# Query split, group norm and the filter's spectrum split on GpSimd instead of VectorE, with other filler pacing, in a kernel for attention and a spectral filter

## The chip, the cores and the metric

The kernel runs on one core of a Trainium2 chip. A core has five engines, each with an instruction stream of its own: TensorE (PE in the profile; its weight loads, PEld, overlap its matmuls), VectorE (DVE), ScalarE (ACT), GpSimd (POOL) and SyncE (SP, which here only issues DMAs). On-chip data lies in SBUF; TensorE writes to PSUM, eight banks of 128 x 512 f32 here. The engines meet through semaphores only, and DMAs move data beside them.

The metric is the device time of one execution in microseconds, the median of several runs. Lower is better.

## What is computed

Two results stand side by side in the output of 2048 rows. On the left is attention with 16 query heads of 28 columns over one shared head of keys and values, then the output projection; on the right a filter in the frequency domain (a two-dimensional real FFT, a product with learned weights, the inverse).

```python
q = (x @ wq).reshape(B, S, H, Dh).transpose(0, 2, 1, 3)    # S 2048, H 16, Dh 28
k = x @ wk
v = x @ wv
scores = jnp.einsum("bhqd,bkd->bhqk", q, k) * (Dh ** -0.5)
p = softmax(scores, axis=-1)
o = jnp.einsum("bhqk,bkd->bhqd", p, v)
a = o.transpose(0, 2, 1, 3).reshape(B, S, H * Dh) @ wo
X = jnp.fft.rfft2(x2, axes=(-2, -1)) * (w_r + 1j * w_i)    # x2 is 2048 x 448
b = jnp.fft.irfft2(X, s=(S, D), axes=(-2, -1))
out = jnp.concatenate([a, b], axis=-1)
```

## The kernel before, in words

**Attention.** The 2048 queries are four chunks c of 512, the 16 heads four groups g of 4, the 2048 keys 16 blocks kc of 128. The main loop has 256 steps, one for each (c, g, kc), in that order. In a step TensorE makes the scores of four heads in two pairs (`scores`, L1257), ScalarE takes the exponential of each pair (L1260, 128 x 1024), and TensorE adds the product with the values into the group's bank (`values`, L1276). Two banks take the groups by turns: the values of a group can't start until VectorE has emptied the bank of the group two before.

**What follows a group.** `group_out` (L1151, VectorE) takes the finished bank out into `qraw`, in the place of the queries that it came from, and GpSimd issues two DMAs that bring the rows of softmax sums through DRAM into `rs` (L1156, L1157). `group_sums` takes the reciprocal (L1161, VectorE) and has GpSimd spread it over `R` (L1162, four L1164). `group_norm` (from L1172) multiplies by `R` and splits the result into a high and a low f16 half, `oh` and `ol`: three VectorE operations of 512 columns. After a chunk's fourth group, SP's DMAs L1184 and L1185 place rows of low parts into spare rows of `oh` and `ol`, and the chunk's output projection (`w_unit`, matmuls L1195, taken out by L1200) may be issued.

**What precedes a group.** `build_q` makes the next group's queries: `split_q` (L207 to L209, three operations of 512 columns) masks them and splits them into f16 halves `qh` and `ql`, then SP writes both to DRAM (L215) and reads them back four times, stacked as the score matmuls want them (L218, `qa`). `split_q` also stands in a branch that these inputs do not take.

**The filter.** Its parts are filler between the attention's steps. On TensorE: the late features and late points of the forward transform (`late_features` out by L1013, `late_points` matmul L1026, out by L1035), then, in the last third, eight spectral products (`z_unit`, L1094), each followed by the last transform (`y_unit`, L1120, out from L1127). Between the two stands VectorE's work on the whole spectrum `X`: a transform over 32 points (`forward`, `inverse`), whose butterflies are pairs of 904 columns (`plain`, L817 and L818), quarter turns (L835 and the four operations behind it, the first of them L837) and general ones (L852, L859), with the product with the filter (L933) in the middle. `X` comes through DRAM: each late point ends in SP's stores t<-bs (`fft1_store`, L196), and after the last one `spectrum` queues the four last loads of `X` (`spread`, L802) on GpSimd, the peak's round trip on SP (`bounce`, L911 and L913, back in L916) and all butterflies as background work of VectorE. After the inverse, `store` (L973) writes `X`, `fft3_load` (L1066) and `fft3_ready` (L1075) bring a product's spectrum and factors in on GpSimd's queue, and `fft3_split` (L1080, L1081) scales and splits the spectrum into f16 halves `c2`, two VectorE operations of 904 columns.

**What sets the order.** Each engine runs its instructions in the order in which they were written, and the kernel writes them by a small model of three clocks (`clk` of TensorE, VectorE, ScalarE). `after(when, dur, f)` books a piece of work: when VectorE's modelled clock has passed `when`, `vector` writes it and moves that clock on by `dur`. Background work is taken where nothing is booked. GpSimd and SP have no clock of their own; what `f` writes on their queues falls in wherever `f` is called. Filler on TensorE is rationed: each step adds to `owed`, and `fill` writes a unit where `owed` is positive. In the early part a step adds the first number of `EARLY`, from the last late point to the opening of the last stage the second, and then what is left spread over the remaining steps. All filler of the early part together, or of the late part, is the same whatever the numbers; they move where it stands.

The prologue (matmul L339, splits such as L533, copies L595, maxima L616) lies ahead of the loop; L1362 and L1365 normalise and split the last group behind it.

## Time and profile before

| | |
|---|---|
| median of 3 runs | 580.23 us (580.09 to 580.28) |
| the profiled execution | 580.55 us, its span 578.8 |
| granted TensorE clock | 0.999 |
| score matmuls L1257 | 4096, 275.5 us |
| value matmuls L1276 | 2048, 268.0 us |
| takings-out of a group, L1151 | 15, 11.3 us, 750 ns each |
| DMA to or from HBM | 44.22 MB read, 19.97 MB written, 111 GB/s |

The profile is of one execution. Busy times of an engine are shares of its span of 578.8 us; the execution's own time is 1.75 us longer than the span. An engine's row gives busy us, share and count of instructions, a group's row count, then busy us and mean ns of one, and behind the bar the idle time ahead of its instructions with what ended it. A timeline row is start, duration, engine, line and operation, with count and idle time ahead; SPq and POOLq are the DMA issues. A window row is the window, its length, then for PE, PEld, DVE, ACT and POOL the busy time (with the number of instructions), then the granted clock, the share of DMA time and its rate in GB/s. A row of the chain is start, duration, engine, tile, line and count.

### The profile page before, as it was taken

What the parts mean: (1) busy time and instruction counts of PE and PEld (TensorE: products, weight loads), DVE (VectorE), ACT (ScalarE), POOL (GpSimd) and SP (SyncE); (2) the same over time, 40 slices, a digit from 0 to 9 for tenths busy, and PEclk for the clock granted to TensorE, in tenths of its full rate; (3) what the DMA queues carried; (4) which work ended last, traced back from release to release, by engine and by line L of the source; (5) the groups of instructions that cost most, each with busy time, mean ns of one, the idle gap of its engine ahead of it and who ended that gap; (6) DMA issues with size and microseconds to landing.
All of it is one profiled execution on the core that took longest, in us unless ns stands there. A gap on an engine that the chain in (4) does not pass through costs nothing.

```text
span 578.8 us, 20617 instructions
## 1 busy us (share of the span) xinstructions
PE 570.6 (99%) x8941; PEld 295.8 (51%) x8941; DVE 390.5 (67%) x747; ACT 513.3 (89%) x580; POOL 102.6 (18%) x187
## 2 busy tenths in 40 slices
PE   9999899999999999999999999999999999999997
PEld 7877454545554444444444444445455555555544
DVE  5996717955421999999898887854366743366544
ACT  3743899999999999999999999998999887898982
POOL 1023311312103011122111111133201221011110
PEclk9999999999999999999999999999999999999999
DMA  8864681625516102242211020467224341212111
GB/s 296 291 212 126 178 267 49 189 84 139 168 35 219 57 19 66 74 123 97 91 34 57 22 79 26 147 220 211 97 89 127 107 131 70 89 58 74 41 56 65
DMA packets 38333, 66.27 MB, mean 115 GB/s; under 512 B 6724, under 2 KB 28532, under 8 KB 38232
## 3 DMA queue, kind: packets, MB, share of 16 engines
q1 hardware_dynamic: 29792, 39.13, 20.9%
q0 software_dynamic: 8304, 25.58, 13.9%
q8 instruction: 70, 1.15, 0.8%
q10 hardware_dynamic: 144, 0.23, 0.1%
q14 instruction: 23, 0.19, 0.1%
HBM read 44.22 MB, written 19.97 MB: 111 GB/s over the span
## 4 chain that ended last, share of the span: by engine, by line
PE 72%; issue 7%; DVE 6%; DMA 3%; POOL 1%; ACT 1%; POOLq 0%; DVEq 0%; ACTq 0%
PE banks L1257 31%; PE banks L1276 30%; PE banks L1195 6%; PE banks L1094 2%; PE banks L1120 2%; DMA rd<-rs 1%; DMA wf<-w 1%; DVE X L817 1%; DVE X L818 1%; DMA R<-rd 1%; PE banks L1026 1%; DVE X L859 1%; PE banks L173 0%; ACT yb L1207 0%; DVE w L852 0%
## 5 line engine op out<-in xcount | busy, mean ns | idle before, releaser
L1260 ACT ACTIVATE p<-banks 128x1024 f32<-128x1024 f32 x512 | 477.4, 1095 | 24.7 <-PE banks L1257 23.4
L1257 PE MATMUL banks<-qa,ka 128*32 128x512 f16 x4096 | 275.5, 379 | 1.6 <-ACT p L1260 1.1
L1276 PE MATMUL banks<-p,vs 128*32 128x512 f32 x2048 | 268.0, 592 | 0.0
L1257 PEld LDWEIGHTS <-ka 128*32 128x32 f16 x4096 | 127.4, 96 | 169.9 <-issue 121.0
L1276 PEld LDWEIGHTS banks<-p,vs 128*32 128x32 f32 x2048 | 68.7, 110 | 44.6 <-issue 1.8
L1156 POOL DMA_DIRECT2D sd<-qraw x15 | 10.1, 676 | 204.5 <-DVE qraw L1151 204.5
L1195 PE MATMUL banks<-woh,o 128*32 128x448 f16 x464 | 39.5, 353 | 0.7 <-DVE X L837 0.7
L1164 POOL DMA_DIRECT2D R<-rd x60 | 30.6, 518 | 42.3 <-DMA rd<-rs 37.0
L1195 PEld LDWEIGHTS <-o 128*32 128x32 f16 x720 | 21.5, 97 | 29.0 <-issue 20.9
L859 DVE SCALAR_TENSOR_TENSOR X<-w,X 128x226 f32<-128x226 f32 (+2 forms) x72 | 34.1, 474 | 2.4
L1151 DVE TENSOR_SCALAR qraw<-banks,scales 128x512 f32<-128x512 f32 x15 | 11.3, 750 | 33.8 <-PE banks L1276 33.8
L1200 DVE TENSOR_SCALAR ya<-banks,scales 128x448 f32<-128x448 f32 x12 | 8.2, 684 | 27.8 <-PE banks L1195 27.8
L1127 DVE TENSOR_SCALAR w<-banks,scales 128x256 f32<-128x256 f32 x16 | 7.8, 484 | 27.3 <-PE banks L1120 27.3
L1162 POOL DMA_DIRECT2D rd<-rs x15 | 8.2, 550 | 92.4 <-DVE rs L1161 83.7
L1195 PE MATMUL banks<-wol,o 128*32 128x448 f16 x256 | 24.0, 352 | 0.0
L339 PE MATMUL banks<-xh,wqh 128*128 128x512 f32 x64 | 23.6, 399 | 0.0
L339 PE MATMUL banks<-xh,wql 128*128 128x512 f32 x64 | 23.0, 389 | 0.0
L343 ACT ACTIVATE qraw<-banks 128x512 f32<-128x512 f32 x16 | 9.3, 594 | 14.8 <-PE banks L339 14.8
L817 DVE TENSOR_TENSOR X<-X 128x904 f32<-128x904 f32 (+2 forms) x10 | 9.1, 906 | 15.6 <-DMA X<-t 15.6
L852 DVE SCALAR_TENSOR_TENSOR w<-X 128x113 f32<-128x113 f32 (+2 forms) x56 | 17.8, 356 | 0.1
L339 PE MATMUL banks<-xl,wqh 128*128 128x512 f32 x48 | 17.2, 390 | 0.0
L933 DVE TENSOR_TENSOR w<-X,wf 128x904 f32<-128x904 f32 x16 | 17.0, 1096 | 0.2
(155 smaller groups left out, 531.5 us busy)
## 6 DMA issues: line engine op xcount, KB each, us to landing
qa<-qd SPq DMA_DIRECT2D x62, 128.0 KB
ob<-yo SPq DMA_DIRECT2D x16, 256.0 KB
t<-bs SPq DMA_DIRECT2D x16, 226.0 KB
w<-w POOLq DMA_DIRECT2D x8, 452.0 KB, 4.7
X<-t POOLq DMA_DIRECT2D x8, 452.0 KB, 7.0
wf<-w POOLq DMA_DIRECT2D x8, 452.0 KB, 5.0
x<-t POOLq DMA_DIRECT2D x8, 452.0 KB, 5.0
R<-rd POOLq DMA_DIRECT2D x60, 56.0 KB, 2.1
```

The lines of the kernel that those rows point to most:

```text
L339: mm(pq[c, g], w[:, j, gs], x[:, j], start=(j == 0 and n == 0), stop=(j == 3 and n == 1))
L817: todo(226 * n, lambda: TT(both(a), both(a), both(b), op=ALU.add), at)
L852: STT(out, y, sy, x, op0=ALU.mult, op1=ALU.add if c > 0 else ALU.subtract)
L859: todo(226 * n, lambda d=d, q=q: STT(both(d), t[0].rearrange("p r n f -> p r (n f)"), q, both(a), op0=ALU.mult, op1=ALU.add))
L933: TT(u[r], both(s), wt[k][:, r:r + 1].to_broadcast([128, 2, 452]), op=ALU.mult)
L1094: mm(pz[r, j], fb["c2", q % 2][:, x, e, j, r], fb["fi", q % 2][:, j, f], start=(n == 0), stop=(n == 2))
L1120: mm(py[m:m + 32, k].rearrange("p (j n) -> p j n", j=4), cs3[:w, kind, f, m:m + 32], fb["z", q % 2, e][:w, x, :, 64 * r:64 * r + 64], star ...
L1164: nc.gpsimd.dma_start(R[32 * i:32 * i + DH], rd[i:i + 1].to_broadcast([DH, CW]))
L1195: mm(p[r:r + 32], x[c][:, g, s][:, r:r + 32], w[:, m], start=(g == 0 and n == 0), stop=(g == NG - 1 and n == 2))
L1257: mm(bank[b + h][r], ka[:, k:k + 32], qa[c, g][:, 2 * p + h], start=True, stop=True)
L1260: nc.scalar.activation(pt[i], banks[:, b:b + 2], AF.Exp, scale=SCALE / UP / UP)
L1276: mm(bank[b][32 * i:32 * i + 32], vs[:, kc], pt[2 * st + i // 2][:, i % 2], start=(kc == 0), stop=(kc == 15))
```

## The change

Three pieces of work are written for GpSimd instead of VectorE. `build_q` hands `split_q` GpSimd as its engine (the branch that isn't taken keeps VectorE). `group_norm` issues its multiply, copy and subtract on GpSimd. `fft3_split` does so too, and in three operations where it had two: the spectrum is scaled in place, then copied to the high half, then subtracted for the low half. None of the three moves VectorE's modelled clock any more (their durations become 0.0), and two delays grow: output projections are released 10 modelled us after a chunk's last norm instead of 7, and a spectral product 6.0 after its split instead of 0.2. `EARLY` goes from 0.22 to 0.18 in its first number, so the early filler is spread over more steps. From `fft3_split` on, a line's number is one higher than before.

```diff
--- before.py
+++ after.py
@@ -33,7 +33,7 @@
 TOP = 61440.0
 ROW = 32768.0
 DUE = 50.0
-EARLY = 0.22, 0.13
+EARLY = 0.18, 0.13
 PEAK = 16384.0
 LAG = 0.45
 BOUND = float(np.float32(40.0 / SCALE * UP * UP / ROW / 4))
@@ -202,11 +202,11 @@
 
     qa, qd = {}, {}
 
-    def split_q(qt, qh, ql, c, g):
+    def split_q(qt, qh, ql, c, g, eng=nc.vector):
         cs = slice(c * CW, (c + 1) * CW)
-        nc.vector.tensor_scalar(qt, qraw[:, g, cs], mask, cvec[:, g, c:c + 1], op0=ALU.mult, op1=ALU.add)
-        nc.vector.tensor_copy(qh, qt)
-        nc.vector.tensor_tensor(ql, qt, qh, op=ALU.subtract)
+        eng.tensor_scalar(qt, qraw[:, g, cs], mask, cvec[:, g, c:c + 1], op0=ALU.mult, op1=ALU.add)
+        eng.tensor_copy(qh, qt)
+        eng.tensor_tensor(ql, qt, qh, op=ALU.subtract)
 
     def stack_out(n, p, src, eng):
         if p == 0:
@@ -220,7 +220,7 @@
     def build_q(c, g):
         qt = qp.tile([128, CW], F32, name="qt")
         qh, ql = (qp.tile([128, CW], F16, name=f"q{n}") for n in "hl")
-        split_q(qt, qh, ql, c, g)
+        split_q(qt, qh, ql, c, g, nc.gpsimd)
         for p, src in enumerate((qh, ql)):
             stack_out(4 * c + g, p, src, nc.sync)
         for p in range(4):
@@ -1073,13 +1073,14 @@
     def fft3_ready(q):
         if q < 8:
             nc.gpsimd.dma_start(fb["fi", q % 2], t["fi"][:, 4 * q:4 * q + 4])
-            after(max(clk["dve"], landed[q]), 2.3, fft3_split, q)
+            after(max(clk["dve"], landed[q]), 0.0, fft3_split, q)
 
     def fft3_split(q):
         x, c2 = fb["x", q % 2], fb["c2", q % 2]
-        V.tensor_scalar(c2[:, 0], x, scale_x, None, op0=ALU.mult)
-        STT(c2[:, 1], x, scale_x, c2[:, 0], op0=ALU.mult, op1=ALU.subtract)
-        after(clk["dve"] + 0.2, 0.0, work["z"].extend, [z_unit(q, 0), z_unit(q, 1)])
+        nc.gpsimd.tensor_scalar(x, x, scale_x, None, op0=ALU.mult)
+        nc.gpsimd.tensor_copy(c2[:, 0], x)
+        nc.gpsimd.tensor_tensor(c2[:, 1], x, c2[:, 0], op=ALU.subtract)
+        after(clk["dve"] + 6.0, 0.0, work["z"].extend, [z_unit(q, 0), z_unit(q, 1)])
         fft3_load(q + 2)
 
     def z_unit(q, e):
@@ -1162,17 +1163,17 @@
         nc.gpsimd.dma_start(rd.rearrange("i (a b) -> (i a) b", b=16), rs)
         for i in range(4):
             nc.gpsimd.dma_start(R[32 * i:32 * i + DH], rd[i:i + 1].to_broadcast([DH, CW]))
-        after(clk["dve"] + 12.0, 2.1, group_norm, c, g)
+        after(clk["dve"] + 12.0, 0.0, group_norm, c, g)
 
     def group_norm(c, g):
         if g == 0:
             parts16 = op.tile([128, 2, NG, CW], F16, name="o16", tag=("oh", "ol")[c % 2])
             oh[c], ol[c] = parts16[:, 0], parts16[:, 1]
         o = osb[c, g]
-        TT(o, o, R, op=ALU.mult)
+        nc.gpsimd.tensor_tensor(o, o, R, op=ALU.mult)
         h = oh[c][:, g]
-        V.tensor_copy(h, o)
-        TT(ol[c][:, g], o, h, op=ALU.subtract)
+        nc.gpsimd.tensor_copy(h, o)
+        nc.gpsimd.tensor_tensor(ol[c][:, g], o, h, op=ALU.subtract)
         normed[c] += 1
         if c < NC - 1:
             if g == 0:
@@ -1183,7 +1184,7 @@
                 for r in range(4):
                     nc.sync.dma_start(oh[c][DH + r::32], rows[r, :, :4])
                     nc.sync.dma_start(ol[c][DH + r::32, 1:], rows[r, :, 4:7])
-                after(clk["dve"] + 7.0, 0.0, work["w"].extend, [w_unit(c, k) for k in range(4)])
+                after(clk["dve"] + 10.0, 0.0, work["w"].extend, [w_unit(c, k) for k in range(4)])
 
     def wo_mm(p, c, k, gs):
         s = slice(k * 128, k * 128 + 128)
@@ -1263,7 +1264,7 @@
         end[i] = clk["act"] + 0.163
         free[b] = free[b + 1] = clk["act"] + 0.153
         if kc == 0 and p == 0 and 4 * c + g < 15:
-            after(clk["pe"] + 3.0, 1.7, build_q, *order[4 * c + g + 1])
+            after(clk["pe"] + 3.0, 0.0, build_q, *order[4 * c + g + 1])
 
     def values(st):
         c, g, kc = steps[st]
```

On VectorE, around the last of the late points (L1035; `bs` is its buffer of points, `spol` that of the features, `peaks` the maxima for the filter's scale), the order before was this. The first row takes out the bank of group (0,2).

```order
L1151 TENSOR_SCALAR qraw<-banks,scales 128x512
L1013 COPY spol<-banks 128x452
L893 TENSOR_REDUCE peaks<-w 128x1
L768 TENSOR_SCALAR woh<-wo,scales 128x448
L1035 COPY bs<-banks 128x4x113
L893 TENSOR_REDUCE peaks<-bs 128x1
L1161 RECIPROCAL rs<-rs 128x16
L905 TENSOR_REDUCE mx<-peaks 128x1
L906 TENSOR_REDUCE mx<-peaks 128x1
L817 TENSOR_TENSOR X<-X 128x2x452
```

The last late point's copy stood four rows behind the taking-out of group (0,2), and the first butterfly, L817, five rows behind that. In the changed kernel the same stretch, from group (0,2) on, reads:

```order
L1152 TENSOR_SCALAR qraw<-banks,scales 128x512
L1035 COPY bs<-banks 128x4x113
L893 TENSOR_REDUCE peaks<-w 128x1
L768 TENSOR_SCALAR woh<-wo,scales 128x448
L1162 RECIPROCAL rs<-rs 128x16
L1013 COPY spol<-banks 128x452
L1152 TENSOR_SCALAR qraw<-banks,scales 128x512
L1035 COPY bs<-banks 128x4x113
L893 TENSOR_REDUCE peaks<-bs 128x1
L905 TENSOR_REDUCE mx<-peaks 128x1
L906 TENSOR_REDUCE mx<-peaks 128x1
L1162 RECIPROCAL rs<-rs 128x16
```

The last L1035 now stands behind the taking-out of group (0,3), the second L1152, and the first butterfly, L817, is the next row behind these.

On GpSimd, from the sums of group (0,2) to those of (0,3), the order before held DMAs only (`t` is the points in DRAM, `wf` the filter's weights):

```order
L1156 DMA sd<-qraw 4x512
L1157 DMA rs<-sd 128x16
L1162 DMA rd<-rs 128x16
L1164 DMA R<-rd 28x512 x4
L802 DMA X<-t_83 128x904 x4
L888 DMA wf<-w 128x904 x2
L1156 DMA sd<-qraw 4x512
L1157 DMA rs<-sd 128x16
```

In the changed kernel, from the sums of group (0,3) on, it is this:

```order
L1157 DMA sd<-qraw 4x512
L1158 DMA rs<-sd 128x16
L207 TENSOR_SCALAR qt<-qraw,mask,cvec 128x512
L208 CAST qh<-qt 128x512
L209 TENSOR_TENSOR ql<-qt,qh 128x512
L802 DMA X<-t_83 128x904 x4
L1163 DMA rd<-rs 128x16
L1165 DMA R<-rd 28x512 x4
L888 DMA wf<-w 128x904 x2
L1173 TENSOR_TENSOR qraw<-qraw,R 128x512
L1175 CAST o_1943<-qraw 128x512
L1176 TENSOR_TENSOR o_1943<-qraw,o_1943 128x512
```

The loads of `X` moved from between groups (0,2) and (0,3) to behind the sums of (0,3), with the split of a group's queries ahead of them and a norm behind them.

On SP, the queue of the same stretch before (`qd` is the queries' halves in DRAM, `md` and `mw` the peak's round trip):

```order
L215 DMA qd<-qh 128x512
L215 DMA qd<-ql 128x512
L218 DMA qa_78<-qd 32x4x512 x4
L196 DMA t_83<-bs 256x1x226 x2
L911 DMA md<-mx 128x2
L913 DMA mw<-md 128x256
L215 DMA qd<-qh 128x512
L215 DMA qd<-ql 128x512
L218 DMA qa_79<-qd 32x4x512 x4
```

And in the changed kernel:

```order
L215 DMA qd<-qh 128x512
L215 DMA qd<-ql 128x512
L218 DMA qa_78<-qd 32x4x512 x4
L215 DMA qd<-qh 128x512
L215 DMA qd<-ql 128x512
L218 DMA qa_79<-qd 32x4x512 x4
L196 DMA t_83<-bs 256x1x226 x2
L911 DMA md<-mx 128x2
L913 DMA mw<-md 128x256
```

The last stores of the points, L196, and the peak's trip behind them moved past the next group's six query DMAs.

## The prediction

> **What bounds the kernel now.** I read the page first: busy shares, the chain, the costliest groups.
>
> ```profile
> PE 570.6 (99%) x8941; PEld 295.8 (51%) x8941; DVE 390.5 (67%) x747; ACT 513.3 (89%) x580; POOL 102.6 (18%) x187
> PE 72%; issue 7%; DVE 6%; DMA 3%; POOL 1%; ACT 1%; POOLq 0%; DVEq 0%; ACTq 0%
> L1260 ACT ACTIVATE p<-banks 128x1024 f32<-128x1024 f32 x512 | 477.4, 1095 | 24.7 <-PE banks L1257 23.4
> ```
>
> TensorE is the chain, and ScalarE's 512 exponentials wait for little but TensorE. VectorE, which the change relieves, is busy 67% and holds 6% of the chain: relief there is worth only what TensorE waits for VectorE. So I went to TensorE's own pace and waits: two rows of the chain, ScalarE's timeline, three windows.
>
> ```profile
> 222.66 0.86 PE banks L1257 x16
> 224.38 0.86 PE banks L1257 x16
> 179.33 43.33 ACT L1260 ACTIVATE p<-banks 128x1024 f32<-128x1024 f32 x47
> 200.00:220.00 20.00, 20.00 (x268) 8.20 (x264) 19.59 (x29) 20.00 (x23) 2.56 (x5) 1.00 0.05 17
> 220.00:240.00 20.00, 19.34 (x288) 8.72 (x286) 19.31 (x45) 19.23 (x21) 4.29 (x8) 1.00 0.19 57
> 440.00:460.00 20.00, 20.00 (x444) 10.93 (x440) 13.22 (x25) 18.04 (x19) 4.11 (x7) 1.00 0.28 98
> ```
>
> One step (scores, then values) takes TensorE 224.38 - 222.66 = 1.72 us without filler. ScalarE needs two exponentials a step, (43.33 - 1.10) / 46 = 0.92 us apart, so 1.84 us. In a stretch without filler ScalarE sets the pace (busy 20.00 of 20) and TensorE loses up to 0.12 us a step; with filler TensorE sets it (440 to 460: ScalarE busy 18.04). All filler is issued anyway, so **the total moves only by what TensorE idles**. One real wait is printed, 0.66 us, in the window from 220:
>
> ```profile
> 222.10 0.37 PE L1195 MATMUL banks<-woh,o 128*32 128x448 f16 x4 [0.66 <-DVE X L837]
> 220.57 0.50 SPq L1185 DMA_DIRECT2D o<-lows  x1
> 220.32 0.74 DVE L1151 TENSOR_SCALAR qraw<-banks,scales 128x512 f32<-128x512 f32 x1
> ```
>
> It is the first piece of chunk 0's output projection, after the values of 83 steps. It needs the rows of o, whose last load was issued at 220.57, and the bank that group (1,0)'s L1151 empties at 221.06. Both kernels have it after step 83.
>
> **The change part by part.** *Filler.* By TensorE's order the last late point stands after step 65, not 53, so 12 steps with idle time get filler: at most 12 x 0.12 = 1.4 us. Part of the 0.92 is small waits for TensorE, so I take **-1.0** (0.5 to 1.4). Output projection and first spectral product keep their order; the product comes after step 177, not 180.
>
> *What VectorE loses.* From its timeline, with the chain that I need next:
>
> ```profile
> 168.00 0.63 DVE L1035 COPY bs<-banks 128x452 f32<-128x452 f32 x1 [3.94 <-PE banks L1026]
> 185.64 1.10 DVE L817 TENSOR_TENSOR X<-X 128x904 f32<-128x904 f32 x1 [15.62 <-DMA X<-t]
> 188.80 0.68 DVE L1172 TENSOR_TENSOR qraw<-qraw,R 128x512 f32<-128x512 f32 x1
> 190.59 1.09 DVE L818 SCALAR_TENSOR_TENSOR X<-X 128x904 f32<-128x904 f32 x1
> 191.60 0.44 DVE L916 TENSOR_REDUCE mx<-mw 128x2 f32<-128x256 f32 x1
> 192.82 0.74 DVE L1151 TENSOR_SCALAR qraw<-banks,scales 128x512 f32<-128x512 f32 x1
> 193.48 0.54 DVE L207 TENSOR_SCALAR qt<-qraw,mask,cvec 128x512 f32<-128x512 f32 x1
> 195.12 1.09 DVE L817 TENSOR_TENSOR X<-X 128x904 f32<-128x904 f32 x1
> 199.41 0.62 DVE L835 COPY w<-X 128x904 f32<-128x904 f32 x1
> 203.11 0.24 DVE L1161 RECIPROCAL rs<-rs 128x16 f32<-128x16 f32 x1
> 204.24 1.09 DVE L817 TENSOR_TENSOR X<-X 128x904 f32<-128x904 f32 x1
> ```
>
> A norm cost VectorE 190.59 - 188.80 = 1.8 us, a split 195.12 - 193.48 = 1.6: 3.4 a group.
>
> *What GpSimd gains.* It ran few such operations:
>
> ```profile
> L1365 POOL TENSOR_TENSOR o<-qraw,o 128x128 f16<-128x128 f32 x3 | 1.3, 425 | 16.7 <-issue 14.0 <-ACT o L1362 2.7
> L1365 DVE TENSOR_TENSOR o<-qraw,o 128x128 f16<-128x128 f32 x1 | 0.3, 293 | 0.0
> 54.88 5.24 POOL L595 COPY qa<-ql 32x512 f16<-32x512 f16 x8 [2.06 <-DVE ql L533]
> 56.64 0.17 DVE L616 SCALAR_TENSOR_TENSOR cmax<-qtop,cmax 128x1 f32<-128x1 f32 x1
> ```
>
> One input, 512 columns: 5.24 / 8 = 0.65. Two inputs: no row at 512, so between 0.65 and 4 x 0.425 = 1.7; the 128 columns take GpSimd 1.45 times VectorE's 0.293, and the norm's three operations average 0.6 on VectorE, so near 1.1, which I take. (The Trainium skill, GPSIMD Engine Reference, section 3.1, gives 4497 ns for 2048 columns; a line from 0.425 at 128 would make it an estimated 1.24. No run here shows it; the sum would grow by 0.3.) A split is then 2.4 us, a norm 2.9, a spectrum split of 904 columns 2 x 1.15 + 1.9 = 4.2. GpSimd has room (18% busy): **its queue counts, not its time**.
>
> *The new wait.* In the order group (0,3)'s L1151 now stands just ahead of the last late point. On GpSimd follow sd, rs, the split of the next queries, and only then the four X loads; on SP the split's qd and qa DMAs now stand ahead of the spectrum's stores t<-bs, which X waits for.
>
> ```profile
> 158.89 0.59 POOL L1156 DMA_DIRECT2D sd<-qraw  x1 [9.14 <-DVE qraw L1151]
> 160.94 0.56 POOL L1157 DMA_DIRECT2D rs<-sd  x1 [1.46 <-DMA sd<-qraw]
> 176.53 2.14 POOL L802 DMA_DIRECT2D X<-t  x4
> 168.66 1.19 SPq L196 DMA_DIRECT2D t<-bs  x2
> 170.05 0.51 SPq L911 DMA_DIRECT2D md<-mx  x1
> 174.09 0.34 SPq L913 DMA_DIRECT2D mw<-md  x1
> 194.51 0.32 SPq L215 DMA_DIRECT2D qd<-qh  x1
> 196.24 1.94 SPq L218 DMA_DIRECT2D qa<-qd  x4
> DMA to landing us min/median/max: 4.5/7.0/10.5
> ```
>
> The last late point's copy was at 168.00; 12 steps of 1.72 to 1.84 put it near 189, less the 1.0 gained: 188. Group (0,3)'s L1151, about a step ahead of it, ends near 186.5. sd to rs takes 2.05, rs 0.56, the split 2.4: 191.5. SP then spends from the split's end (195.2) to 198.18 on qd and qa, 3.0: 194.5. From the stores to the landing of the small DMA behind them was 174.09 - 168.66 = 5.4, an upper end; the lower is a small DMA's 2.05; I take 4.2: X issued at 198.7. From X to the first butterfly passed 185.64 - 176.53 = 9.1 (6.1 to 12.1 by the least and greatest landing of the last load, issued 1.6 later): 207.8. Ahead of (1,0)'s L1151 stand four butterfly pairs, the scale and a quarter turn: (199.41 - 195.12) x 2 + (192.82 - 191.60) + (204.24 - 199.41 - 0.2) = 14.4, and the copy out, 0.74: **the bank is free at 223.0**. TensorE arrives at 222.10 - 0.66 - 1.0 = 220.4. It waits 2.6, where it waited 0.66: **+1.9** (-0.7 with the fastest loads and stores, when the old wait goes too, to +5). Behind that piece stand all scores, and ScalarE runs dry.
>
> *Both engines on SBUF at once.* Beside these 14 us GpSimd runs a norm and a split, 5.3 us. If VectorE stood still for all of it the wait grows by 5.3; if not, by nothing. L616 above, with two SBUF inputs, took its usual 0.17 beside a running GpSimd copy, so I stay near nothing: **+0.4**. (The Trainium skill, SBUF — State Buffer, section "Who interferes with whom": a VectorE instruction with two SBUF inputs and a GpSimd one that reads SBUF exclude each other, and the later one is blocked entirely. Nearly all butterflies have two. That one-element row does not show it; by the rule the sum gets +5.3 here and more later, a rival below.)
>
> *First spectral product.* Its slack:
>
> ```profile
> 383.14 0.77 POOL L973 DMA_DIRECT2D t<-X  x1
> 391.93 0.55 POOL L1075 DMA_DIRECT2D fi<-fi  x1
> 398.44 1.16 DVE L1081 SCALAR_TENSOR_TENSOR c<-x,scales,c 128x904 f16<-128x904 f32 x1
> 404.12 0.86 PE L1094 MATMUL banks<-fi,c 128*32 128x128 f16 x48
> ```
>
> Before, c was ready at 399.60 and used at 404.12. The store at 383.14 stays behind the same R loads on GpSimd, whatever VectorE does. After the fi load GpSimd now has a norm (2.9) and the split (4.2): 392.5 + 7.1 = 399.6. TensorE comes three steps earlier, 404.12 - 5.2 + 1.3 = 400.2. It just fits; **+0.3** (0 to 3). The other splits and norms have most of a 30 us group to spare.
>
> **Sum:** -1.0 + 1.9 + 0.4 + 0.3 = +1.6 us. The profiled execution took 580.55 (span 578.8), 0.3 above the median 580.23; from the median, **581.8**.
>
> **The rivals.** *Faster.* The wait at step 83 vanishes if X lands some 3 us sooner than reckoned; for it speaks the spread of 4.5 to 10.5, against it that four X loads run together. Then -1.0 - 0.66: **578.6**, chance 0.16. *Nothing measurable,* the change not doing what it says: the relief is real but the shorter idle and the longer wait cancel, 579.1 to 581.4; chance 0.24, most of it the lower part of my own case. *Much slower by exclusion.* GpSimd's 5.3 us a group stand against 3.4 removed, so the spectrum's VectorE work, with six groups in it, ends up to 6 x 5.3 = 32 us later than without exclusion. From about 4 us of delay on, the first spectral product waits. A third of it, 11 us, less the slack, with +3 at step 83: **590**; whole, over 600. Against it stands L616, for it only the rule; chance 0.26.
>
> **How the numbers follow.** My case, 579.5 to 585, has 0.58 with its lower part; 0.16 faster; 0.26 exclusion. About 0.2% (1.2 us) is what a measurement can tell from no change. Faster 0.16, same 0.24, slower 0.60. The range reaches from the faster rival to the middle of exclusion: 578.6 to 592.
>
> **What would show it.** Right: TensorE's first L1195 with an idle of 2 to 4 us released by VectorE near 223; L817 starting near 208; the last t<-bs behind qa<-qd; VectorE's busy time down by some 65 us. Exclusion: L818, L859 or GpSimd's own durations stretched against 1.10 us, and idle ahead of L1094. Wrong: no idle at step 83, or GpSimd's two-input operations far from 1.1 us.

## The result and the profile after

The changed kernel takes **610.51 us** (median of 4 runs, 609.25 to 611.65), the kernel before beside it 580.25 (580.09 to 580.58): a ratio of 1.0511, interval 1.0494 to 1.0528. That is 30 us slower, far above the forecast of 581.8 and above its range, which ended at 592. The profiled execution took 611.1 us, its span 609.3 (before: 580.55 and 578.8).

The page of the changed kernel, busy shares and chain:

```profile
PE 578.6 (95%) x8941; PEld 296.8 (49%) x8941; DVE 353.7 (58%) x641; ACT 514.7 (84%) x580; POOL 244.2 (40%) x301
PE 48%; DVE 16%; POOL 11%; DMA 8%; issue 5%; SPq 1%; ACT 1%; POOLq 0%; DVEq 0%; ACTq 0%
```

VectorE did get rid of work (390.5 to 353.7 us), GpSimd took 142 us more, and TensorE, with the same 8941 matmuls, fell from 72% to 48% of the chain. The span grew by 30.5 us. Of this 22.5 are idle time of TensorE (609.3 - 578.6 against 578.8 - 570.6), and 8.0 are longer busy time for the same matmuls. The first part is in the list of TensorE's waits (who waited for whom, then total us, times, longest):

```profile
PE banks L1196 <- DVE qraw L1152: 9.1, 1, 9.1
PE banks L1196 <- DMA o<-lows: 5.3, 1, 5.3
PE banks L1095 <- POOL c L1081: 4.1, 1, 4.1
PE banks L1121 <- DVE w L1130: 1.8, 1, 1.8
PE banks L1095 <- POOL c L1082: 1.7, 1, 1.7
PE banks L1095 <- DVE ya L1201: 1.4, 1, 1.4
```

Before, the only entry above 0.5 us behind the loop's first step was the 0.7 at L1195. Now there are three places: the first output projection (9.1), the first spectral product and its neighbours (4.1, 1.7, 1.4, 1.8), and the projection of chunk 2 (5.3).

Most of the second part shows in the granted clock. Windows around the first wait (third figure from the end is the clock):

```profile
221.00:224.00 3.00, 0.00 (x0) 0.00 (x0) 2.96 (x4) 1.09 (x2) 2.85 (x3) 1.00 0.09 28
224.00:227.00 3.00, 0.00 (x0) 0.10 (x1) 2.97 (x3) 0.00 (x0) 1.04 (x1) 0.68 0.31 103
227.00:230.00 3.00, 0.01 (x4) 0.01 (x3) 2.97 (x5) 0.00 (x0) 0.00 (x0) 0.50 0.56 168
230.00:234.00 4.00, 4.00 (x32) 1.44 (x35) 3.93 (x6) 1.94 (x2) 1.18 (x2) 0.50 0.02 6
234.00:236.00 2.00, 2.00 (x26) 0.80 (x21) 1.93 (x5) 0.70 (x1) 0.00 (x0) 0.68 0.03 4
236.00:240.00 4.00, 4.00 (x65) 1.81 (x61) 3.96 (x6) 3.54 (x5) 0.32 (x1) 1.00 0.00 0
```

TensorE is idle from 220.9 to 230.0. The clock falls to half some 4 us into the idle time and is back only after about 5 us of work, near 235.3, so 4.0 x 0.50 + 2.0 x 0.32 = 2.6 us of work are lost behind the wait. The same happens behind the waits at 411 to 417 (2.8 us lost) and at 498 (1.7), 7.1 us in all. Where the other 0.9 of the 8.0 us lie was not followed up.

Two of the long chains show in the timelines. SP's queue (start, duration) around the stores of the last points:

```profile
191.34 0.34 SPq L215 DMA_DIRECT2D qd<-qh  x1
192.59 1.10 SPq L215 DMA_DIRECT2D qd<-ql  x1
194.54 1.78 SPq L218 DMA_DIRECT2D qa<-qd  x4
196.42 1.19 SPq L196 DMA_DIRECT2D t<-bs  x2
```

The points were copied by 189.14, but their stores stood behind the queries' DMAs, which waited for GpSimd's split: 7 us lost before `X` could be loaded. VectorE from there on:

```profile
211.07 1.10 DVE L817 TENSOR_TENSOR X<-X 128x904 f32<-128x904 f32 x1 [19.11 <-DMA X<-t]
218.41 1.14 DVE L925 SCALAR_TENSOR_TENSOR scales<-mx 128x1 f32<-128x1 f32 x1
221.60 1.47 DVE L818 SCALAR_TENSOR_TENSOR X<-X 128x904 f32<-128x904 f32 x1
223.95 2.04 DVE L837 TENSOR_TENSOR X<-X 128x904 f32<-128x904 f32 x1
229.19 0.74 DVE L1152 TENSOR_SCALAR qraw<-banks,scales 128x512 f32<-128x512 f32 x1
```

The same L818 took 1.10 where nothing ran beside it, and L837 1.09 in the kernel before; L925, an operation on one column, took 1.14 instead of 0.15. From the first butterfly to the free bank it took 18.9 us (229.93 - 211.07).

GpSimd's queue between the last sums and the last norm of chunk 2:

```profile
465.87 0.57 POOL L1158 DMA_DIRECT2D rs<-sd  x1 [2.44 <-DMA sd<-qraw]
467.00 2.56 POOL L1080 TENSOR_SCALAR x<-x,scales 128x904 f32<-128x904 f32 x1
469.63 0.93 POOL L1081 CAST c<-x 128x904 f16<-128x904 f32 x1
470.65 1.92 POOL L1082 TENSOR_TENSOR c<-x,c 128x904 f16<-128x904 f32 x1
473.66 0.56 POOL L1163 DMA_DIRECT2D rd<-rs  x1
479.39 2.04 POOL L1165 DMA_DIRECT2D R<-rd  x4 [5.17 <-DMA rd<-rs]
481.99 2.57 POOL L1080 TENSOR_SCALAR x<-x,scales 128x904 f32<-128x904 f32 x1
...
489.25 1.29 POOL L1173 TENSOR_TENSOR qraw<-qraw,R 128x512 f32<-128x512 f32 x1
```

One split stands between the sums and their way back to DRAM (rs was there by 468.48, when VectorE took its reciprocal), a second one between `R` and the norm. The rows of `o` are then issued from 492.49 on, and TensorE stands from 492.7 to 498.06.

### The profile page after: what moved, and what is told of

Read it like the earlier page. It is cut to its first block, busy times and chain, and to the rows that moved or that the text cites. A ratio compares the mean times of both kernels' runs of the same rounds, so it can differ in the third digit from the quotient of the medians.

```text
span 609.3 us, 20615 instructions
## 1 busy us (share of the span) xinstructions
PE 578.6 (95%) x8941; PEld 296.8 (49%) x8941; DVE 353.7 (58%) x641; ACT 514.7 (84%) x580; POOL 244.2 (40%) x301
## 3 DMA queue, kind: packets, MB, share of 16 engines
q8 instruction: 70, 1.15, 0.8%
## 4 chain that ended last, share of the span: by engine, by line
PE 48%; DVE 16%; POOL 11%; DMA 8%; issue 5%; SPq 1%; ACT 1%; POOLq 0%; DVEq 0%; ACTq 0%
PE banks L1258 21%; PE banks L1277 20%; PE banks L1196 4%; POOL x L1080 3%; DVE X L859 2%; DVE X L864 2%; DMA rd<-rs 2%; POOL c L1082 2%; DMA sd<-qraw 2%; DVE w L933 2%; DMA t<-X 1%; DVE X L825 1%; DVE w L852 1%; DVE X L823 1%; DMA X<-t 1%
## 5 line engine op out<-in xcount | busy, mean ns | idle before, releaser
L1196 PE MATMUL banks<-woh,o 128*32 128x448 f16 x464 | 41.4, 367 | 14.5 <-DVE qraw L1152 9.1
L859 DVE SCALAR_TENSOR_TENSOR X<-w,X 128x226 f32<-128x226 f32 (+2 forms) x72 | 40.5, 562 | 2.3
L1152 DVE TENSOR_SCALAR qraw<-banks,scales 128x512 f32<-128x512 f32 x15 | 11.2, 749 | 42.9 <-PE banks L1277 42.9
L1173 POOL TENSOR_TENSOR qraw<-qraw,R 128x512 f32<-128x512 f32 x15 | 20.8, 1389 | 23.7 <-DMA R<-rd 23.6
L1103 DVE TENSOR_SCALAR z<-banks 113x512 f16<-113x512 f32 (+1 forms) x16 | 11.0, 690 | 25.9 <-PE banks L1095 25.8
L486 POOL DMA_DIRECT2D kf<-qraw x12 | 6.2, 522 | 44.5 <-ACT qraw L343 44.5
L1128 DVE TENSOR_SCALAR w<-banks,scales 128x256 f32<-128x256 f32 x16 | 7.7, 478 | 25.8 <-PE banks L1121 25.8
L1095 PE MATMUL banks<-fi,c 128*32 128x128 f16 (+2 forms) x768 | 14.4, 224 | 7.2 <-POOL c L1081 4.1
```

The source lines that it names most:

```text
L859: todo(226 * n, lambda d=d, q=q: STT(both(d), t[0].rearrange("p r n f -> p r (n f)"), q, both(a), op0=ALU.mult, op1=ALU.add))
L1095: mm(pz[r, j], fb["c2", q % 2][:, x, e, j, r], fb["fi", q % 2][:, j, f], start=(n == 0), stop=(n == 2))
L1173: nc.gpsimd.tensor_tensor(o, o, R, op=ALU.mult)
L1196: mm(p[r:r + 32], x[c][:, g, s][:, r:r + 32], w[:, m], start=(g == 0 and n == 0), stop=(g == NG - 1 and n == 2))
```

## Experiments

Each run's own time stands beside runs of the kernel before on the same chip; ratios are with their 95% interval. The expectations weigh theories against each other: O puts the loss down to the order in the queues, E to the exclusion (GpSimd and VectorE holding each other up at SBUF) and what it delays, P to the pacing, C is about the clock.

### Each part by itself

Pacing alone is this edit:

```diff
-EARLY = 0.22, 0.13
+EARLY = 0.18, 0.13
```

> The kernel before with the first number of EARLY at 0.18 and nothing else. Theory O (order: the time was lost because stores and loads of X stood behind GpSimd's split of the queries): without a split on GpSimd the stores follow the last late point at once, X is issued near 194 and the first butterfly behind it stands near 202 instead of 211, so TensorE waits under 1 us at the first output projection. Theory E (both engines on SBUF exclude each other): no compute is on GpSimd, so no butterfly is stretched, L859 stays at 474 ns. Neither sees a wait at step 83. But VectorE keeps all its work and starts the spectrum 16 us later, so the first spectral product comes some 15 to 20 us later than 404 and a remainder may stand at the end: 579.2 if it all still fits, up to 587 if not.

The queries alone:

```diff
-        split_q(qt, qh, ql, c, g)
+        split_q(qt, qh, ql, c, g, nc.gpsimd)
...
-            after(clk["pe"] + 3.0, 1.7, build_q, *order[4 * c + g + 1])
+            after(clk["pe"] + 3.0, 0.0, build_q, *order[4 * c + g + 1])
```

> The kernel before with only the split of the next queries on GpSimd (EARLY as before). The last late point stays near 168. Theory O: X is loaded as before, first butterfly near 185.6, no wait over 1 us at the first output projection, 579.5 to 581. Theory E: six splits of 2.5 us stand beside the spectrum and stretch VectorE's butterflies (L859 from 474 to over 500 ns) and are stretched by them (L207 over 0.9 us mean); the bank of group (1,0) is late by 2 to 4 us at the first output projection and TensorE's clock falls behind that wait: 583 to 587.

The norms alone:

```diff
-        TT(o, o, R, op=ALU.mult)
+        nc.gpsimd.tensor_tensor(o, o, R, op=ALU.mult)
...
-                after(clk["dve"] + 7.0, 0.0, work["w"].extend, [w_unit(c, k) for k in range(4)])
+                after(clk["dve"] + 10.0, 0.0, work["w"].extend, [w_unit(c, k) for k in range(4)])
```

> The kernel before with only the norm of the groups on GpSimd and the output projection's release at 10 instead of 7. Theory O: the butterflies keep their durations, the inverse ends some 10 us earlier than 382, and the first spectral product is planned earlier; at most a wait of 1 to 2 us there: 579.5 to 582. Theory E: five or six norms of 3.1 us stretch the butterflies (L859 over 500 ns) and the inverse ends only some 4 us earlier; 581 to 585 with a wait of 2 us or more at a projection or at the first product.

The filter's split alone is the hunk of `fft3_ready` and `fft3_split`.

> The kernel before with only the split of the filter's spectrum on GpSimd. The spectrum itself is untouched: L859 at 474 ns, inverse ends at 382 by both theories. Theory O (GpSimd's queue): a split takes 5.4 us there and the R loads of a norm stand behind it, so VectorE waits for R and TensorE for a product or a projection: 582 to 587. Theory E: only VectorE operations with two SBUF inputs suffer and there are few in the last third (L1138, the norms), so 580 to 581.5.

| kernel | median us | before us | ratio | TensorE's waits |
|---|---|---|---|---|
| pacing alone | 586.59 | 580.76 | 1.0087 (1.0061 to 1.0112) | 1.2; 2.2 and 0.9 at the end |
| queries alone | 587.75 | 580.76 | 1.0118 (1.0077 to 1.0159) | 3.5, 0.6 |
| norms alone | 586.04 | 580.76 | 1.0090 (1.0063 to 1.0117) | 3.4 |
| filter's split alone | 590.59 | 580.76 | 1.0161 (1.0121 to 1.0201) | 6.7, 0.7 |

Every part loses by itself, and each for a reason of its own. *Pacing* gains up to the last group and then has products left over: the late spectrum (first product at 430.3, not 404.1) leaves 7.7 us of them, waits included, behind the loop (562.6 to 570.2). The wait at step 83 was 1.2 us, a little over what was said, and the time is at the upper end. *Queries*: 3.5 us at the first projection, as theory E had it (L859 took 515 ns, L207 970), though for the rows of `o` and not for the bank; the time is 0.8 us over its range. *Norms*: the time is over both ranges, by 1.0 us over theory E's. The inverse ended 13 us earlier (368.84), nearer to theory O's 10, and yet the exclusion was there: L859 took 521 ns, and the durations of the spectrum's 302 operations add up to 177.5 us instead of 162.3. Two things made up for it: the 11 us of norms were gone, and so were 13.5 us in which VectorE, in its old order, stood among these operations waiting for banks from TensorE (L1151 6.3, L1200 7.2). But the order had booked the first product's split too early; VectorE stood 13.6 us before `x` with an output row behind it, for whose bank TensorE waited:

```profile
385.92 0.69 DVE L1080 TENSOR_SCALAR c<-x,scales 128x904 f16<-128x904 f32 x1 [13.62 <-DMA x<-t]
...
389.93 0.68 DVE L1200 TENSOR_SCALAR ya<-banks,scales 128x448 f32<-128x448 f32 x1
```

*The filter's split* decides for theory O and its queue. GpSimd, then VectorE:

```profile
409.30 1.91 POOL L1082 TENSOR_TENSOR c<-x,c 128x904 f16<-128x904 f32 x1
412.28 0.58 POOL L1163 DMA_DIRECT2D rd<-rs  x1
420.82 2.05 POOL L1165 DMA_DIRECT2D R<-rd  x4 [7.96 <-issue]
```

```profile
424.58 0.69 DVE L1173 TENSOR_TENSOR qraw<-qraw,R 128x512 f32<-128x512 f32 x1 [7.11 <-DMA R<-rd]
427.54 0.47 DVE L1128 TENSOR_SCALAR w<-banks,scales 128x256 f32<-128x256 f32 x1
```

The DMAs of a norm stand behind two splits on GpSimd, the norm stands in VectorE's order waiting for `R`, the taking-out L1128 stands behind the norm, and TensorE waits 6.7 us for it. L859 stayed at 474 ns. The place is theory O's; the time is 3.6 us over its range.

### The exclusion by itself

The kernel before, with work on a scratch tile added on GpSimd behind each group's R loads, once reading SBUF and once only writing it:

```diff
+        for _ in range(3):
+            nc.gpsimd.tensor_tensor(pr, pr, pr, op=ALU.add)
```

> The kernel before with three additions of 128 x 512 on a scratch tile of its own on GpSimd behind each group's R loads (3 x 1.2 to 1.3 us; nothing waits for them, they add work that the result does not use). Theory E: each blocks VectorE's two-input operations and is blocked by them; L859 rises over 510 ns, the inverse ends 8 to 20 us later than 382, the first spectral product late with a wait and a slow clock behind it: 584 to 598. Theory O (only order and queue matter): L859 stays at 474 ns, the additions lie in GpSimd's free time: 580 to 581.

```diff
+        for _ in range(7):
+            nc.gpsimd.memset(pr, 0.0)
```

> As the probe with additions, but seven memsets of the same 128 x 512 tile (about 0.52 us each, 3.6 us a group): GpSimd is as long busy and only writes SBUF. If the exclusion needs GpSimd to read SBUF: L859 at 474 ns and 580 to 581. If a running GpSimd instruction is enough: as the probe with additions, L859 over 510 ns and 584 or more.

With additions 589.61 us, ratio 1.0146 (1.0132 to 1.0161); with memsets 586.46, 1.0091 (1.0077 to 1.0106); before 580.86. The groups of VectorE's butterflies, with additions and then with memsets:

```profile
L859 DVE SCALAR_TENSOR_TENSOR X<-w,X 128x226 f32<-128x226 f32 (+2 forms) x72 | 35.5, 493 | 2.4
L933 DVE TENSOR_TENSOR w<-X,wf 128x904 f32<-128x904 f32 x16 | 19.4, 1246 | 0.2
L864 DVE SCALAR_TENSOR_TENSOR X<-w,X 128x226 f32<-128x226 f32 (+1 forms) x32 | 15.5, 544 | 0.3
```

```profile
L859 DVE SCALAR_TENSOR_TENSOR X<-w,X 128x226 f32<-128x226 f32 (+2 forms) x72 | 34.1, 473 | 2.4
L933 DVE TENSOR_TENSOR w<-X,wf 128x904 f32<-128x904 f32 x16 | 17.0, 1096 | 0.2
L864 DVE SCALAR_TENSOR_TENSOR X<-w,X 128x226 f32<-128x226 f32 (+1 forms) x32 | 12.4, 446 | 0.3
```

Beside additions they grow (before: 474, 1096 and 446), beside memsets of a like total length (56.1 us, the additions 52.4) they don't. Added up over the trace, the durations of all 302 operations on the spectrum were 162.3 us before, 163.0 beside memsets and 181.8 beside additions. So GpSimd's reading, not its running, holds VectorE up. The Trainium skill, SBUF — State Buffer, section "Who interferes with whom", says just this of a VectorE instruction with two SBUF inputs; the trace agrees. What was not expected: L859 stayed under the 510 ns that were named, since the stretch fell on other lines, and **the memsets cost 5.6 us too**. Next to nothing was stretched there (one copy L835 of 113 columns took 0.67 us, its twin 0.21). TensorE's wait at the first projection, 0.7 us before, was 4.3 us (with additions 7.7), for the rows of `o`, whose way leads over GpSimd's queue, and the loads of `X` were issued from 181.0 on (with additions from 180.4) instead of 176.5. Occupying the queue cost more than the exclusion added, 3.2 us.

### Parts together, and one taken back

> The changed kernel with the first number of EARLY back at 0.22. The last late point returns to about 168 and X to about 185. Theory P (pacing put the stores and loads of X behind the split, and that is most of the loss): no wait over 1 us at the first output projection, 585 to 592. Theory E (exclusion and GpSimd's own queue): the 9.1 us shrink only to the 3 to 4 us of the run with the queries alone, since the norm that feeds the rows of o still stands late on GpSimd; the inverse ends 20 to 30 us earlier than 391, and TensorE waits 4 us or more for the first spectral product, whose split takes 5.4 us on GpSimd; each of these waits is followed by a halved clock: 594 to 602.

> The kernel before with the norm on GpSimd, the release at 10, and EARLY at 0.18: the change without its two splits. The last late point comes near 189 as in the changed kernel, but nothing but DMAs stands ahead of the loads of X on GpSimd. Theory P: X lands near 202, no wait over 0.5 us at the first projection, the late start of the spectrum is made up by the norms taken off VectorE (the run with the norms alone ended the inverse 13 us earlier), so the first product comes near 405 and all filler fits: 578.9 to 579.7, ahead of both kernels. Theory E: norms still stretch the butterflies (L859 near 520 ns), the inverse ends at 386 or later and the product waits: 581 to 586.

> The changed kernel with the filter's split back on VectorE (norms, queries and pacing as changed). Every theory leaves the first wait of 9 us with its slow clock. If GpSimd's 5.4 us per split is what made the last third late, the waits at the first product (4.1 and 1.7), at its successors (1.4 and 1.8) and for the rows of chunk 2 (5.3) shrink to 3 us or less in sum and one slow clock remains: 594 to 600. If the late spectrum is what counts there (it ends at 391 either way), the product still waits some 5 us, now for VectorE: 600 to 606.

> The changed kernel with the split of the queries back on VectorE (norms, filter split and pacing as changed): the run with norms and pacing (581.9) and the filter's split on GpSimd added. If the queries' split is what turned a loss of 1 us into one of 30, with the filter's split only worth its own wait: no wait over 1 us at the first projection, one wait of 3 to 7 us in the last third with its slow clock: 585 to 592. If the parts simply add up (+9.8 for the filter's split alone): 590 to 593. Over 595 would say that the filter's split, not the queries, is the larger share.

| kernel | median us | before us | ratio |
|---|---|---|---|
| norms, pacing | 581.86 | 580.86 | 1.0031 (1.0018 to 1.0044) |
| norms, pacing, filter's split | 594.27 | 581.09 | 1.0223 (1.0185 to 1.0262) |
| norms, pacing, queries | 598.37 | 581.09 | 1.0300 (1.0276 to 1.0324) |
| norms, queries, filter's split | 603.14 | 580.86 | 1.0371 (1.0354 to 1.0388) |
| all of the change | 610.51 | 580.25 | 1.0511 (1.0494 to 1.0528) |

Norms and pacing mend each other: 11.1 us lost apart, 1.0 together, in theory E's range (L859 502 ns, the inverse ends at 387.8). The likely reason, argued and not shown, is that the late spectrum is made up by the relief and the early product by the late spectrum. The two splits don't: on top of norms and pacing the queries cost 16 us and the filter's split 12, together 29. With the queries away there is no wait at the first projection at all; its waits are 7.1 at a product (VectorE stood 9.6 us before rs, whose DMA on GpSimd stood behind a filter's split), 2.2 at products behind it and 2.7 for rows. With the filter's split away 8.6 and 6.1 remain, the second because VectorE stood 13.8 us before the late `x`: the time is in the first range of the expectation, the wait in the second. The expectation for the kernel without the queries (at most 592, or 593 by adding up) was too low by 1 to 2 us. With the old pacing the first wait is 3.6 us and the first product waits 7.0, both as theory E had it; the rows of chunk 2 still come 3.2 us late, and the time is 1.1 us over its range.

### The place on SP

The changed kernel, with one number:

```diff
-            after(clk["pe"] + 3.0, 0.0, build_q, *order[4 * c + g + 1])
+            after(clk["pe"] + 10.0, 0.0, build_q, *order[4 * c + g + 1])
```

> The changed kernel with the split of the next queries booked 10 instead of 3 modelled us after a group's first scores; VectorE's order is the same row for row. On SP the last stores of the points now stand ahead of the next group's six query DMAs. Theory O (the stores' place on SP made X late): stores follow the last late point within 2 us (about 189 to 191 instead of 196.4), the first butterfly stands near 203 to 205 instead of 211, group (1,0)'s bank is free near 222 to 224, the first wait falls from 9.1 to 1 to 4 us, and the spectrum ends 6 to 8 us earlier with the product's wait unchanged in size: 600 to 606. Theory E (the first wait is mostly exclusion and the late rows of o): the stores move, the wait stays at 6 us or more: 607 to 611.

604.97 us, ratio 1.0417 (1.0400 to 1.0433). SP, VectorE and TensorE of this kernel:

```profile
188.40 1.19 SPq L196 DMA_DIRECT2D t<-bs  x2
```

```profile
205.91 1.10 DVE L817 TENSOR_TENSOR X<-X 128x904 f32<-128x904 f32 x1 [14.85 <-DMA X<-t]
222.81 0.74 DVE L1152 TENSOR_SCALAR qraw<-banks,scales 128x512 f32<-128x512 f32 x1
```

```profile
PE banks L1196 <- DVE qraw L1152: 4.8, 4, 3.3
```

Most of theory O's numbers came: stores 8 us earlier, the bank free at 223.6, the first wait 3.3 (the largest of four) instead of 9.1. The first butterfly was 0.9 us later than its range, and the spectrum ended 4.6 us earlier (386.7), not 6 to 8. So some 6 of the 9 us were the stores' place on SP and what followed from it; what is left is in the main the exclusion in front of the bank, which came 17.6 us behind the first butterfly, against 15.2 reckoned without it. The later waits stayed (that for the rows of chunk 2 grew from 5.3 to 6.5), and with them 24 us.

### The clock by itself

The kernel before, with reductions whose result is unused ahead of the taking-out of group (1,0), two or four of them:

```diff
+        for _ in range(4 if (c, g) == (1, 0) else 0):
+            V.tensor_reduce(dm, X[:, 0, 0:8], axis=AX.XY, op=ALU.max)
```

> The kernel before with two reductions of 904 columns (1.09 us each, their result unused) put on VectorE just ahead of the taking-out of group (1,0), so that its bank comes 2.2 us later. TensorE's wait at the first projection, 0.66 us, becomes 2.3 to 2.9. Theory C (a wait costs its length, and from about 3.4 us on also some microseconds at half clock): no window with a granted clock under 1.00 behind it, time up by 1.6 to 2.4 us: 582.4 to 583.4 beside a before of 580.8. Without such an edge, if every wait costs 2.5 us more than its length: 585.

> The same with four reductions, the bank 4.4 us later, the wait 4.4 to 5.2 us. Theory C: the granted clock falls to 0.50 behind the wait for 4 to 6 us, which costs 2 to 3 us more than the wait's growth of 3.8 to 4.5: 586.5 to 588.5 beside a before of 580.8. If the clock costs nothing: 584.6 to 585.3.

Two: 581.64 against 580.64, ratio 1.0013 (1.0004 to 1.0022), 0.8 us under theory C's range, with a wait of 2.3 us in the profiled execution, which took 582.45. Four: 586.80, ratio 1.0093 (1.0076 to 1.0111), a wait of 4.5. Windows behind the wait, with two and with four:

```profile
224.00:226.00 2.00, 2.00 (x32) 0.95 (x35) 1.93 (x7) 0.94 (x2) 0.60 (x1) 1.00 0.56 165
226.00:228.00 2.00, 2.00 (x36) 0.89 (x32) 1.93 (x5) 2.00 (x4) 0.00 (x0) 1.00 0.37 109
```

```profile
224.00:226.00 2.00, 0.00 (x0) 0.00 (x0) 1.97 (x3) 0.00 (x0) 0.00 (x0) 0.81 0.41 115
226.00:228.00 2.00, 1.46 (x16) 0.69 (x19) 1.93 (x6) 0.00 (x0) 0.60 (x1) 0.50 0.54 162
230.00:232.00 2.00, 2.00 (x24) 0.62 (x16) 1.93 (x6) 0.52 (x2) 0.49 (x1) 0.50 0.05 4
```

2.2 us more of wait cost 5.2 us more of time. The clock stayed at 1.00 behind the wait of 2.3 and was at half until 232 behind that of 4.5. But there is no edge in the length of the wait: in the other runs the clock fell behind waits of 2.7 us (rows of `o`, the changed kernel with its queries back on VectorE), 3.2 (rows of chunk 2, old pacing), 3.4, 3.5 and 3.6 (norms alone, queries alone, first wait with the old pacing), and stayed up behind one of 3.3 (queries later).

The clock's own records in the traces tell more. Ahead of the programs' ends there are 20 stretches at half clock, and each lasts 3.41, 6.83 or 10.24 us, that is one, two or three times 3.41. Within one execution they all begin and end on one grid of 3.41 us, which lies elsewhere in another execution. Two windows of that grid, the first with the wait of 2.7, the second with the wait of 3.3:

```profile
475.38:478.79 3.41, 0.84 (x20) 0.59 (x24) 0.00 (x0) 1.12 (x2) 3.03 (x3) 1.00 0.46 169
218.92:222.33 3.41, 1.43 (x20) 0.43 (x16) 3.34 (x4) 2.66 (x3) 0.00 (x0) 1.00 0.06 20
```

In the first TensorE is idle for 3.41 - 0.84 = 2.57 us, and the clock is at half from 478.79 on. In the second it is idle for 1.98, the rest of the wait falls into the next window, and the clock stays up. From the loop's start on, in all traces, it fell behind each such window with 2.09 us of idle time or more and behind only one of those with 2.01 or less (1.99); it came back behind windows with 0.59 or less and behind none with 0.92 or more. This is read from the traces; no run moved a wait along the grid. By these figures, as an estimate, a single wait under 2 us leaves the clock alone, one of more than 4 us halves it wherever it falls, and between them its place decides. The Trainium skill, TensorE: Matmul & The Clock Gate, Part 1, gives an idle window of about 3.4 us that runs freely, so that its place is not fixed. Length and grid agree with that, but here a window needn't be idle throughout.

### GpSimd's slow multiply, and what can be kept

> The kernel before with eight operations on scratch tiles added on GpSimd behind the norm DMAs of group (0,1), results unused; their durations count, not the time. L1080 took 2.55 us for 904 columns, L207 0.76 for 512. If the multiply with one scalar from SBUF is slow whatever the size of the tile: about 2.5 at 904 and 1.5 at 512, in place or not. If a second scalar operand makes it fast: 1.2 to 1.3 at 904 and 0.76 at 512 with two scalars. If f32 from an immediate is the cheap form: near the cast's 0.94 at 904.

Eight forms on scratch tiles behind the DMAs of group (0,1). L1171 is L1080's form, L1172 has its scalar as a constant, L1173 a second multiply by a scalar from SBUF; L1174 and L1175 are the first and third on 512 columns:

```profile
143.23 2.54 POOL L1171 TENSOR_SCALAR ga<-ga,mask 128x904 f32<-128x904 f32 x1 [0.15 <-issue]
145.86 2.73 POOL L1172 TENSOR_SCALAR ga<-ga 128x904 f32<-128x904 f32 x1
148.70 1.09 POOL L1173 TENSOR_SCALAR ga<-ga,mask 128x904 f32<-128x904 f32 x1
149.89 1.56 POOL L1174 TENSOR_SCALAR ga<-ga,mask 128x512 f32<-128x512 f32 x1
151.54 0.77 POOL L1175 TENSOR_SCALAR ga<-ga,mask 128x512 f32<-128x512 f32 x1
```

The form with one operation takes more than twice as long as that with two, at either size. In place or not makes no difference (2.54 into f16).

> The run with norms and pacing, with the filter's split booked for 18 instead of 9 modelled us after the load's issue. There VectorE stood 5.6 us before the split waiting for x, with the output rows ya behind it, and TensorE waited 0.9 and 1.2 us. Expected: the output rows come ahead of the split, both waits vanish, what is left is the 1.1 us that pacing gains before the first projection: 579.3 to 580.3, against 580.9 before. If instead the later product overfills the end: 581 to 584.

581.40 against 581.09, ratio 1.0007 (0.9993 to 1.0021), in the second range: all waits but one of 0.7 us are gone, and still nothing is gained. The last exponentials start 0.4 us ahead of before, the end is 0.2 ahead: the lead is 2.8 us at the start of the thirteenth group, when less filler is done than before, and melts from there. That the steps without filler up to the later product (415.1 instead of 404.1) gave the gain back is argued, not shown.

> The kernel before with the first number of EARLY at 0.19, nothing on GpSimd. The spectrum starts some 8 us later than before instead of 22 us as with 0.18, so the products still fit: early gain of about 1 us by the first projection. If it is kept: 579.6 to 580.3 beside 580.8. If it is given back at the end as in the run with norms and the later product: 580.5 to 581.2.

579.37 against 580.64, ratio **0.9983** (0.9974 to 0.9992). With 0.19 the spectrum ends at 384.5 and the first product stands at 407.1, 3 us later than before, the wait at the first projection is gone, none above 0.5 us is left behind the loop's first step, and the early gain is kept: 1.3 us. It is the only version faster than the kernel before, and it moves nothing to GpSimd.

## Why the prediction was wrong, step by step

- **What bounds the kernel**, that only TensorE's idle time counts: right, but for the clock. Waits of the changed kernel were priced at their length. Behind 9.1, 5.8 and 5.3 us the clock halves and costs another 7.1 us in all. No step had such a term.
- **Filler, -1.0**: right. TensorE reached the first projection at 230.0 - 9.1 = 220.9 (said: 220.4), in an execution whose loop began 0.5 us later.
- **The new wait at step 83, 2.6 us**: the right place, the right chain and the right queues, the wrong size. The split ended at 192.6 (said: 191.5), the stores were issued at 196.4, the first loads of `X` at 200.3 (198.7) and the first butterfly ran at 211.1 (207.8): 3.3 us by small terms and a slow landing. From there to the free bank it took 18.9 us (15.2): 3.7 by exclusion. That the norm which feeds the rows of `o` also stood behind the loads of `X` on GpSimd (its last operation ended at 219.5) was not reckoned at all.
- **Both engines on SBUF, +0.4**: this step failed most plainly. The value was taken near nothing because of L616, a row that could not tell: the copy beside it ended 0.01 us before L616 did, so there was nothing left to wait for. The row fits the exclusion as well: in the changed kernel L925, also of one column, ended 0.02 us behind the GpSimd operation beside it. The durations of the spectrum's operations grew from 162.3 to 185.2 us in sum, and the probe shows the cause; for this reason too VectorE's busy time fell by 36.8 us and not by the 65 foretold. Of the rival with exclusion (590, whole: over 600) the mechanism was right; its upper end of 32 us in six groups stands against 22.9 measured. But exclusion alone did not make the 30 us.
- **First spectral product, +0.3**: failed. Its data was there at 417.3 (said: 399.6), TensorE was there at 411.3. The inverse ended at 391.25 instead of 382 and the store had to wait for four R loads on GpSimd until 397.07; norm and split behind the load took 8.7 us (said: 7.1), of which the slow multiply was 2.54 instead of 1.15.
- **"The other splits and norms have most of a 30 us group to spare"**: failed. GpSimd had the time (40% busy), but its order did not: at 467 to 473 the way back of the sums stood behind one split (5.6 us), at 482 to 488 the norm stood behind the next (6.1), and the rows of chunk 2 came 5.3 us late. The prediction itself said that GpSimd's queue counts and not its time, and then weighed the queue at two places only.
- **GpSimd's prices**: 1.15 to 1.30 for two inputs of 512 columns where it ran undisturbed (said: 1.1), 0.61 for a copy (0.65); only the multiply of 904 columns was far off.

What these runs leave open is how many of the 30 us are exclusion and how many are order, since a late spectrum makes the queues collide in other places. The nearest figures, neither of them a bound, are the probes (in the kernel before, exclusion adds 3.2 us to the queue's 5.6) and the run with the stores in their old place (24 us of loss remain).

## What to carry to other kernels

An engine that issues the DMAs of a chain is not free because it is idle four fifths of the time: whatever is put on its queue delays every issue behind it, so follow each of its DMAs to who waits for it before moving compute there, also where only scratch is written. Work moved from VectorE to GpSimd is paid for in part by VectorE's own operations with two SBUF inputs, which stop for GpSimd's reads, and by some with one: beside GpSimd's cast the copy L835 of 904 columns took 1.03 us instead of 0.62. Those that read PSUM, and reductions, kept their times here (L1152 749 ns against 750, L893 1085 against 1086). Price a single wait of TensorE by its length only up to about 2 us; from there on it can halve the clock, which cost another 1.4 to 3.1 us each time here, and above 4 us it always did.

## What was not expected of the hardware

On GpSimd a `tensor_scalar` with one operation took 2.54 us for 904 columns, with two operations 1.09; 1.56 and 0.77 for 512. The exclusion holds for operations of a single column too: L925, which scales the peak, took 0.15 us before, and 1.14 beside GpSimd's copy and subtraction of the norm, with whose end it ended. L917, one input of two columns, took 0.82 instead of 0.17. A wait of 2.7 us halved TensorE's clock where one of 3.3 us did not.
